# Weight loads in written order through the attention, 4,864-byte record rows, and output scatters that no longer wait for each other

## The chip, the cores and the metric

The kernel runs on one core of one Trainium2 chip. The metric is the device time of one execution in microseconds (us). Engines are named as in the profile: PE is TensorE, PEld its weight loads, DVE VectorE, ACT ScalarE, POOL GpSimd, SP SyncE, which only issues transfers here. "L157" is line 157 of the kernel before.

## The reference

Two stages. The first is attention over 8 batches, 12 heads, 448 positions and 64 dimensions with RMS-normalised q and k. The second is a mixture of 8 experts over the 3,584 token rows of 768 values that the attention gives: each row passes a dense two-layer network and one expert, chosen by its largest logit and scaled by that expert's softmax weight.

```python
q_n, k_n = rmsnorm(q, g_q), rmsnorm(k, g_k)
attn = softmax(q_n @ k_n.T / 8)            # per batch and head
x = (attn @ v) as rows (batch, position) of 768
y = relu(x @ w1_dense) @ w2_dense
e = argmax(x @ w_gate);  p = softmax(x @ w_gate)[e]
y += p * (relu(x @ w1[e]) @ w2[e])
```

## The kernel before

**Attention (to about 348 us).** The work is cut into 48 pieces t, each of two heads of one batch, six to a batch; two pieces make a group g of four heads. `load(g)` fetches q and k of a group (448 KB each, issued by SP, L137) and v (issued by POOL, with a cast to bf16, L141) into three buffers each. `squares(t)` multiplies x by itself on POOL (L157), and DVE sums the squares (L158). ACT makes the scale r of the group, `normalise(t)` applies it on DVE (L173), and `transposes(t)` turns q and k with PE (L182). `scores(t, j)` makes four blocks of scores with PE (L198), and ACT exponentiates each (L200): four such activations are one piece. `attend` multiplies by v (L211), and DVE divides into the row tile `xa` (L217). `values(g)` copies v into its own tile on DVE (L148).

One loop over t mixes these: scores of t+1, transposes of t+2, squares of t+4, normalise of t+3, load of group t/2+3 at each even t. Between them it works off, a few matmuls at a time, the dense network of the batch before (`dense1`, L265, `dense2`, L276). At the end of a batch `route(b)` makes the logits and writes the batch's rows to a table "records" in DRAM (L255, L256); `dense2` writes the dense result of each row beside them (L285).

The expert weights are 16 loads (`wjobs[3:]`, L321), two per expert, issued by POOL with a cast from float32 to bf16 (768 KB each after it). The loop names them at t = 3, 5, 8, 10, 13 and so on to 40:

```python
while nw < len(wjobs) and (nw - 2) * 5 <= t * 2:
    nc.gpsimd.dma_start(*wjobs[nw])
    nw += 1
```

The order on the engines is made by a scheduler ahead of time: only PE keeps the written order (`tc.manual_schedule(engines={PE})`). On the other engines, SP's and POOL's transfers among them, the scheduler puts forward what it holds to be ready; each engine then works through its list in that order, and an instruction that waits holds up all behind it.

**Dispatch (348 to 373 us).** DVE works out the slot of each token: 35 tiles of 128 slots, each tile of one expert.

**Experts (from 373 us).** For tile t, `gather(t)` fetches its 128 rows from the records (POOL, indirect, L441) into `xg`, which has five buffers. PE transposes them (L452), multiplies by the first weights (L461), transposes again (L471) and multiplies by the second (L479). DVE adds the dense result of the same record into `ys` (L485), and POOL scatters the 128 rows to the output (indirect, L487). Gather t+5 needs the buffer that the addition of tile t frees. The scatters all write one DRAM tensor at rows that are known only at run time, so the tracking of dependencies makes each wait until the one before has landed.

A row of the records is 385 float32 words (768 bf16 values and one word with the gate) and 768 words of the dense result: 1,153 words, 4,612 bytes.

Of the kernel before, what the change touches and what calls it, by code (L numbers as in the profile page):

```python
# [8 lines left out]
F32 = mybir.dt.float32  # L9
BF16 = mybir.dt.bfloat16  # L10
# [7 lines left out]
def kernel(  # L18
# [14 lines left out]
    nc = tc.nc  # L33
    P = 128
    B, H, S, D = q.shape
    N = B * S
    Dm = H * D
# [3 lines left out]
    SC = S // JJ  # L41
# [23 lines left out]

    EB = E * KD * F
    NTL = N // P + E - 1
    RW = Dm + 2
    NC4 = 4 * B
    tri = const.tile([P, P], BF16)  # L70
    ones = const.tile([P, P], BF16)
# [30 lines left out]
        nc.vector.tensor_copy(tok[:, b, :, 2], colp)  # L102
    nc.vector.memset(tok[:D, :, 3, :], 0.0)

    RC = RW // 2 + Dm
    rec = nc.dram_tensor("records", (N, RC), F32).ap()
    oh = const.tile([P, B, 4, E], BF16)
    wgb = const.tile([P, KD, E], BF16)
# [13 lines left out]
    with tc.tile_pool(name="a_ld", bufs=3) as ld, \  # L122
         tc.tile_pool(name="a_sb", bufs=2) as sb, \
         tc.tile_pool(name="a_sc", bufs=2, space=bass.MemoryType.PSUM) as scp, \
         tc.tile_pool(name="a_wk", bufs=4, space=bass.MemoryType.PSUM) as wkp:
        xin, ssqs, rs, xn, qkT, exs, vas, xnats, xTs, hTs, vrs = [{} for _ in range(11)]

        def load(g):
# [73 lines left out]
        def attend(t, hh):  # L202

            b, pr = divmod(t, NPR)
            if pr == 0 and hh == 0:
                xnats[b] = sb.tile([P, 4, RW], BF16, tag="xa", name="xa")
                xTs[b] = sb.tile([P, NPR, S], BF16, tag="xT", name="xT")
            av = wkp.tile([P, 4, De], F32, tag="wk", name="av")
            for mi in range(4):
                for j in range(JJ):  # L210
                    nc.tensor.matmul(av[:, mi], exs[t][:, j, hh, QC[mi]:QC[mi] + P],  # L211
                                     vas[t // GP][:, 2 * (t % GP) + hh, j, :De],
                                     start=(j == 0), stop=(j == JJ - 1))
            inv = sb.tile([P, 4, 1], F32, tag="inv")
            nc.vector.reciprocal(inv, av[:, :, D:])
            h = 2 * pr + hh
            nc.vector.tensor_mul(xnats[b][:, :, h * D:(h + 1) * D], av[:, :, :D],  # L217
                                 inv.to_broadcast([P, 4, D]))
# [11 lines left out]
        def route(b):  # L230

            lp = wkp.tile([P, 4, E], F32, tag="wk", name="tr")
            for mi in range(4):
                for kk in range(KD):
                    nc.tensor.matmul(lp[:, mi], xTs[b][:, kk, QC[mi]:QC[mi] + P], wgb[:, kk, :],
                                     start=(kk == 0), stop=(kk == KD - 1))
            mx = sb.tile([P, 4, 1], F32, tag="mx")
            nc.vector.tensor_reduce(mx, lp, AX.X, ALU.max)
            cent = sb.tile([P, 4, E], F32, tag="cent")
            nc.vector.tensor_sub(cent, lp, mx.to_broadcast([P, 4, E]))  # L240
            eg = sb.tile([P, 4, E], F32, tag="eg")
            nc.scalar.activation(eg, cent, AF.Exp)

            hot = sb.tile([P, 4, E], F32, tag="hot")
            nc.vector.scalar_tensor_tensor(hot, in0=cent, scalar=0.0,
                                           in1=prio.unsqueeze(1).to_broadcast([P, 4, E]),
                                           op0=ALU.is_equal, op1=ALU.mult)
            m2 = sb.tile([P, 4, 1], F32, tag="m2")
            nc.vector.tensor_reduce(m2, hot, AX.X, ALU.max)
            nc.vector.tensor_tensor(oh[:, b], hot, m2.to_broadcast([P, 4, E]), ALU.is_equal)  # L250
            sm = sb.tile([P, 4, 1], F32, tag="sm")
            nc.vector.tensor_reduce(sm, eg, AX.X, ALU.add)
            nc.vector.reciprocal(xnats[b][:, :, Dm:].bitcast(F32), sm)
            dst = rec[b * S:b * S + 3 * P, :RW // 2].rearrange("(m p) w -> p m w", p=P)
            nc.sync.dma_start(dst, xnats[b][:, :3].bitcast(F32))  # L255
            nc.sync.dma_start(rec[b * S + 3 * P:(b + 1) * S, :RW // 2], xnats[b][D:, 3].bitcast(F32))  # L256


        def dense1(b, ff, part, n=3):
# [10 lines left out]
        def dense2(b, j, dd, part, n=2):  # L270
            if part == 0:
                if dd == 0:
                    ffs[1] = sb.tile([SC, 2, Dm // 2], F32, tag="ys", name="ys")
                ffs[0] = wkp.tile([SC, Dm // 2], F32, tag="wk", name="ff")
            for ff in range(part * FT // n, (part + 1) * FT // n):
                nc.tensor.matmul(ffs[0], hTs[b][:, ff, j * SC:(j + 1) * SC],  # L276
                                 wd2[:, ff, dd * Dm // 2:(dd + 1) * Dm // 2],
                                 start=(ff == 0), stop=(ff == FT - 1))
            if part == n - 1:
                if dd == 0:  # L280
                    nc.scalar.copy(ffs[1][:, dd], ffs[0])
                else:
                    nc.vector.tensor_copy(ffs[1][:, dd], ffs[0])
                    r0 = b * S + j * SC
                    nc.sync.dma_start(rec[r0:r0 + SC, RW // 2:],  # L285
                                      ffs[1].rearrange("p a d -> p (a d)"))

        ffs = [None, None]
# [8 lines left out]
                for f, *args in PIECES[n * len(PIECES) // NSL:(n + 1) * len(PIECES) // NSL]:  # L297
                    f(b - 1, *args)

        with tc.manual_schedule(engines={mybir.EngineType.PE}):  # L300
            for g in range(3):
                load(g)
            for job in wjobs[:3]:
                nc.gpsimd.dma_start(*job)
            for t in range(2 * GP):
                squares(t)
            values(0)
            for t in range(3):
                normalise(t)
            for t in range(2):  # L310
                transposes(t, "q")
                transposes(t, "k")
            for j in range(JJ):
                scores(0, j)
            nw = 3
            for t in range(NT + NPR):
                if t < NT:
                    if t % GP == 0:
                        load(t // GP + 3)
# [3 lines that stand above are left out]
                for i in range(4):  # L323
                    if t + 1 < NT:
                        scores(t + 1, i)
                    if i % 2 == 0:
                        if t + 2 < NT:
                            transposes(t + 2, "qk"[i // 2])
                        if i == 2 and 0 < t <= NT:
                            xtrans(t - 1)  # L330
                    elif t < NT:
                        attend(t, i // 2)
                    dense(t, i)
                    if i < 2:
                        if t + 2 * GP < NT:
                            squares(t + 2 * GP, "qk"[i])
                    elif t + 3 < NT:
                        normalise(t + 3, "qk"[i - 2])
                    if i == 3 and t % GP == GP - 1 and t + 1 < NT:
                        values((t + 1) // GP)  # L340

    with tc.tile_pool(name="m_sb", bufs=5) as sb, \
# [94 lines left out]
        xgs = {}  # L437
# [8 lines left out]
        xTs, hes, heTs = {}, {}, {}  # L446

        def xtrans(t):
            xb = xgs[t][:, :Dm // 2].bitcast(BF16)
            xp = ps1.tile([P, KD, P], BF16, tag="tr")  # L450
            for kk in range(KD):
                nc.tensor.transpose(xp[:, kk], xb[:, kk * P:(kk + 1) * P], ident)  # L452
            xTs[t] = sb.tile([P, KD, P], BF16, tag="xT", name="xT")
            nc.vector.tensor_copy(xTs[t], xp)  # L454

        def gemm1(t):
            gate = xgs[t][:, Dm // 2:RW // 2]
            eregs[t] = nc.tensor.value_load(tei[:, t:t + 1], min_val=0, max_val=E - 1)
            he = ps2.tile([P, F], F32, tag="he")
            for kk in range(KD):  # L460
                nc.tensor.matmul(he, xTs[t][:, kk],  # L461
                                 we[:, bass.ds(eregs[t], 1), 0, kk * F:(kk + 1) * F]
                                 .rearrange("p o f -> p (o f)"),
                                 start=(kk == 0), stop=(kk == KD - 1))
            hes[t] = sb.tile([P, F], BF16, tag="hs", name="hs")
            nc.scalar.activation(hes[t], he, AF.Relu, scale=gate)  # L466
# [8 lines left out]
        def gemm2(t):  # L475
            yp = psy.tile([P, 2, 512], F32, tag="y")
            for ff in range(FT):
                for dd in range(2):
# [4 lines left out]
                                     start=(ff == 0), stop=(ff == FT - 1))  # L483
            ys = sb.tile([P, 2, HD], F32, tag="ys")
            nc.vector.tensor_add(ys, yp[:, :, :HD],  # L485
                                 xgs[t][:, RW // 2:].rearrange("p (a d) -> p a d", a=2))
            nc.gpsimd.indirect_dma_start(  # L487
                out=out, out_offset=bass.IndirectOffsetOnAxis(ap=dest[:, t:t + 1], axis=0),
                in_=ys.rearrange("p a d -> p (a d)"), in_offset=None,
                bounds_check=N - 1, oob_is_err=False)  # L490

        eregs = {}
        for t in range(4):
            gather(t)
        with tc.manual_schedule(engines={mybir.EngineType.PE}):
# [44 lines left out]
```

## Time and profile before

| | us |
|---|---|
| median of 3 runs (lowest, highest) | 540.01 (537.35, 541.17) |
| the profiled execution | 539.3 |
| its span in the profile | 537.3 |

The span is the time from the first to the last instruction of the profiled execution; 2.0 us lie around it. All stretches below are in us from the start of the span. Mean granted clock of TensorE over it: 0.903 of 2.4 GHz.

### The profile page before, as it was taken

To read this page: it belongs to the slowest core of one execution; us is meant where nothing else is said; L and a number is where in the kernel's file an instruction comes from. 1 tells how busy PE (TensorE), PEld (TensorE's weight loads), DVE (VectorE), ACT (ScalarE), POOL (GpSimd) and SP (SyncE) were. 2 spreads that over 40 slices of the span, in tenths; PEclk is the share of its full clock that TensorE was granted. 3 is DMA by queue.
4 is the path that set the end of the run, shared out by engine and by line. 5 is a ranking of instruction groups with operands and counts; after the bars stand their busy time and mean duration, and the time that the engine had idled before them with its cause. 6 is when DMAs were issued, how large, how long until landed. Compare 5 with 4: busy or idle time off the path is not lost. (4 is left out here: it accounts for less than half of the span.)

```text
span 537.3 us, 10725 instructions
## 1 busy us (share of the span) xinstructions
PE 401.6 (75%) x3995; PEld 232.5 (43%) x4010; DVE 319.0 (59%) x759; ACT 273.8 (51%) x431; POOL 207.1 (39%) x223
## 2 busy tenths in 40 slices
PE   0198891769889898888898999802597877878882
PEld 0155550445454454554554656502254444445441
DVE  3899780968977786786887854275143433334331
ACT  0088582557677777776778888300132333223320
POOL 6785542625433444343333000001244544444432
PEclk9998586788898999898899999956699999899997
DMA  8999999999576465555563312410556766677650
GB/s 149 236 243 233 235 241 238 217 266 234 118 169 149 111 165 139 135 142 138 138 154 107 93 63 73 144 43 8 213 177 201 234 228 196 207 239 230 232 180 26
DMA packets 62176, 90.58 MB, mean 169 GB/s; under 512 B 4909, under 2 KB 52269, under 8 KB 62128
## 3 DMA queue, kind: packets, MB, share of 16 engines
q0 software_dynamic: 31568, 51.36, 41.2%
q1 hardware_dynamic: 30560, 38.56, 25.0%
q8 instruction: 33, 0.54, 0.4%
q14 instruction: 15, 0.12, 0.1%
HBM read 82.03 MB, written 30.29 MB: 209 GB/s over the span
## 5 line engine op out<-in xcount | busy, mean ns | idle before, releaser
L200 ACT ACTIVATE ex<-ps 112x896 bf16<-112x896 f32 x192 | 174.0, 921 | 60.0 <-PE ps L198 59.1
L198 PE MATMUL ps<-y 64*112 64x448 bf16 x384 | 84.4, 437 | 3.8 <-ACT ex L200 2.1
L158 DVE TENSOR_REDUCE ssq<-sq 112x8 f32<-112x512 f32 x96 | 64.3, 673 | 34.3 <-POOL sq L157 34.2
L157 POOL TENSOR_TENSOR sq<-xq 112x512 f32<-112x512 f32 x48 | 50.8, 1058 | 84.0 <-DMA xq<-in_q_dram 51.9
L211 PE MATMUL av<-va,ex 112*128 112x65 bf16 x1536 | 71.2, 202 | 11.5 <-DVE xa L217 8.7
L276 PE MATMUL ff<-wd,hT 128*112 128x384 bf16 x256 | 62.4, 356 | 15.8 <-DVE xa L217 15.6
L211 PEld LDWEIGHTS <-ex 112*128 112x128 bf16 x1536 | 59.1, 103 | 34.0 <-issue 20.7
L441 POOL DMA_INDIRECT xg<-records,row x35 | 33.9, 968 | 91.7 <-DVE dest L434 81.3
L487 POOL DMA_INDIRECT out_dram<-ys,dest x35 | 35.7, 1019 | 79.4 <-DVE ys L485 28.5
L157 POOL TENSOR_TENSOR sq<-xk 112x512 f32<-112x512 f32 x48 | 54.0, 1125 | 30.1 <-DMA xk<-in_k_dram 15.4
L454 DVE COPY xT<-xp 128x768 bf16<-128x768 bf16 x35 | 19.5, 558 | 73.8 <-PE xp L452 69.8
L182 PE MATMUL tr<-ident,y 112*128 112x112 bf16 x384 | 39.7, 233 | 27.1 <-DVE y L173 24.5
L473 ACT COPY heT<-hp 128x512 bf16<-128x512 bf16 x35 | 20.5, 585 | 69.3 <-PE hp L471 69.3
L466 ACT ACTIVATE hs<-he,xg 128x512 bf16<-128x512 f32 x35 | 24.1, 687 | 62.3 <-DMA xg<-records,row 35.5
L198 PEld LDWEIGHTS <-y 64*112 64x112 bf16 x384 | 26.5, 132 | 63.1 <-issue 51.2
L479 PE MATMUL yp<-we,heT 128*128 x280 | 52.3, 331 | 0.8 <-DVE ys L485 0.8
L461 PE MATMUL he<-we,xT 128*128 x195 | 50.5, 384 | 2.8 <-DVE xT L454 0.8
L265 PE MATMUL ff<-xT,wd 128*128 128x448 bf16 x192 | 50.6, 367 | 2.6 <-DVE xa L217 2.6
L485 DVE TENSOR_TENSOR ys<-yp,xg 128x768 f32<-128x768 f32 x35 | 33.5, 958 | 28.9 <-PE yp L479 28.9
L182 PEld LDWEIGHTS <-y 112*128 112x128 bf16 x384 | 22.8, 105 | 49.8 <-DVE y L173 27.3
L173 DVE TENSOR_TENSOR y<-xq,r 112x512 bf16<-112x512 f32 x48 | 42.5, 886 | 0.8 <-ACT r L164 0.7
L452 PE MATMUL xp<-ident,xg 128*128 128x128 bf16 x210 | 18.6, 228 | 31.5 <-DMA xg<-records,row 23.4
(97 smaller groups left out, 490.1 us busy)
## 6 DMA issues: line engine op xcount, KB each, us to landing
we<-in_moe_w_dram POOLq DMA_DIRECT2D x16, 768.0 KB, 33.5
records<-ys SPq DMA_DIRECT2D x32, 336.0 KB, 3.6
xq<-in_q_dram SPq DMA_DIRECT2D x23, 448.0 KB, 6.1
xk<-in_k_dram SPq DMA_DIRECT2D x23, 448.0 KB, 5.7
vr<-in_v_dram POOLq DMA_DIRECT2D x24, 224.0 KB, 4.9
records<-xa SPq DMA_DIRECT2D x8, 577.5 KB, 4.1
wd<-in_moe_w_dense_dram POOLq DMA_DIRECT2D x2, 768.0 KB
records<-xa SPq DMA_DIRECT2D x8, 96.2 KB, 4.4
```

The source lines that it names most:

```text
L157: nc.gpsimd.tensor_mul(sq, x, x)
L158: nc.vector.tensor_reduce(ssqs[g][:, n, 2 * i * JJ:(2 * i + 2) * JJ], sq.rearrange("p h (j d) -> p (h j) d", d=D), AX.X, ALU.add)
L173: nc.vector.tensor_mul(y.rearrange("p j h d -> p h j d"), x.rearrange("p h (j d) -> p h j d", d=D), rs[g][:, n, 2 * i * JJ:(2 * i + 2) * J ...
L182: nc.tensor.transpose(ps[:, j * SC:(j + 1) * SC], xn[name, t][:, j].rearrange("p h d -> p (h d)"), ident[:SC, :SC])
L198: nc.tensor.matmul(ps[:, hh, :S], qkT["k", t][d0:d0 + D, j * SC:(j + 1) * SC], qkT["q", t][d0:d0 + D, :], start=True, stop=True)
L200: nc.scalar.activation(exs[t][:, j], ps[:, :, :S], AF.Exp, scale=scale)
L211: nc.tensor.matmul(av[:, mi], exs[t][:, j, hh, QC[mi]:QC[mi] + P], vas[t // GP][:, 2 * (t % GP) + hh, j, :De], start=(j == 0), stop=(j == ...
L265: nc.tensor.matmul(ffs[0], wd1[:, kk, ff * P:(ff + 1) * P], xTs[b][:, kk], start=(kk == 0), stop=(kk == KD - 1))
L276: nc.tensor.matmul(ffs[0], hTs[b][:, ff, j * SC:(j + 1) * SC], wd2[:, ff, dd * Dm // 2:(dd + 1) * Dm // 2], start=(ff == 0), stop=(ff == F ...
L461: nc.tensor.matmul(he, xTs[t][:, kk], we[:, bass.ds(eregs[t], 1), 0, kk * F:(kk + 1) * F] .rearrange("p o f -> p (o f)"), start=(kk == 0), ...
L479: nc.tensor.matmul(yp[:, dd, :HD], heTs[t][:, ff], we[:, bass.ds(eregs[t], 1), 1, ff * Dm + dd * HD:ff * Dm + (dd + 1) * HD] .rearrange("p ...
L487: nc.gpsimd.indirect_dma_start(out=out, out_offset=bass.IndirectOffsetOnAxis(ap=dest[:, t:t + 1], axis=0), in_=ys.rearrange("p a d -> p (a ...
```

## The change

- SP and POOL join PE in the manual schedule of the attention: their instructions, transfers too, are issued as the loop writes them. The weight loads so go out at t = 3, 5, 8, ..., 40.
- A record row becomes 384 words of x, 768 words of the dense result, and 64 words whose first is the gate: 1,216 words, 4,864 bytes. x, the dense result and the tail begin at bytes 0, 1,536 and 4,608 of the row.
- The gate is no longer part of the `xa` tile. It goes into one of two small tiles `gt`, and `route` writes their 256-byte rows with two transfers more per batch (16 in all).
- Each output scatter is declared free of the earlier ones.

```diff
-    RW = Dm + 2
+    XH = Dm // 2
+    GO = XH + Dm
...
-    RC = RW // 2 + Dm
+    RC = Dm // 2 + Dm + 64
...
+        gts = [sb.tile([P, 4, RC - GO], F32, name=f'gt{i}', tag=f'gt{i}', bufs=1) for i in range(2)]
+        for gt in gts:
+            nc.vector.memset(gt, 0.0)
...
-                xnats[b] = sb.tile([P, 4, RW], BF16, tag="xa", name="xa")
+                xnats[b] = sb.tile([P, 4, Dm], BF16, tag="xa", name="xa")
...
-            nc.vector.reciprocal(xnats[b][:, :, Dm:].bitcast(F32), sm)
-            dst = rec[b * S:b * S + 3 * P, :RW // 2].rearrange("(m p) w -> p m w", p=P)
-            nc.sync.dma_start(dst, xnats[b][:, :3].bitcast(F32))
-            nc.sync.dma_start(rec[b * S + 3 * P:(b + 1) * S, :RW // 2], xnats[b][D:, 3].bitcast(F32))
+            gt = gts[b % 2]
+            nc.vector.reciprocal(gt[:, :, :1], sm)
+            r3 = b * S + 3 * P
+            nc.sync.dma_start(rec[b * S:r3, :XH].rearrange("(m p) w -> p m w", p=P),
+                              xnats[b][:, :3].bitcast(F32))
+            nc.sync.dma_start(rec[r3:r3 + D, :XH], xnats[b][D:, 3].bitcast(F32))
+            nc.sync.dma_start(rec[b * S:r3, GO:].rearrange("(m p) w -> p m w", p=P), gt[:, :3])
+            nc.sync.dma_start(rec[r3:r3 + D, GO:], gt[D:, 3])
...
-                    nc.sync.dma_start(rec[r0:r0 + SC, RW // 2:],
+                    nc.sync.dma_start(rec[r0:r0 + SC, XH:GO],
...
-        with tc.manual_schedule(engines={mybir.EngineType.PE}):
+        with tc.manual_schedule(engines={mybir.EngineType.PE, mybir.EngineType.Pool, mybir.EngineType.SP}):
...
-            nc.gpsimd.indirect_dma_start(
+            i = nc.gpsimd.indirect_dma_start(
                 out=out, out_offset=bass.IndirectOffsetOnAxis(ap=dest[:, t:t + 1], axis=0),
...
+            for j in stores:
+                tc.declare_no_dep(i.ins, j.ins, reason="each token has one slot")
+            stores.append(i)
```

The expert stage reads the parts of a record at their new places; its schedule is as before (PE alone in written order).

## Rows read from the trace of the kernel before

**Rows 1.** Busy time by stretch: engines' busy us (instructions), granted clock, DMA share, GB/s.

```profile
20.00:95.00 75.00, 54.12 (x564) 31.80 (x564) 54.11 (x121) 45.16 (x68) 39.28 (x43) 0.80 1.18 237
130.00:260.00 130.00, 113.27 (x1309) 64.17 (x1308) 102.24 (x262) 96.11 (x155) 53.96 (x53) 0.93 0.59 141
399.00:520.00 121.00, 96.78 (x671) 54.43 (x681) 43.40 (x57) 36.21 (x57) 56.73 (x57) 0.99 0.66 220
```

**Rows 2.** The activations of L200 by stretch: ACT busy (count), clock, DMA share, GB/s.

```profile
55.00:126.00 71.00, 29.44 (x33) 0.72 1.18 240
126.00:268.00 142.00, 79.95 (x89) 0.93 0.61 146
```

**Rows 3.** PE in order of time, 81.8 to 96 us: start, length, line, [idle before].

```profile
82.13 0.68 PE L211 MATMUL av<-va,ex 112*128 112x65 bf16 x16
95.28 0.89 PE L276 MATMUL ff<-wd,hT 128*112 128x384 bf16 x2 [12.47 <-DVE xa L217]
```

**Rows 4.** DVE in order of time, 85 to 95 us.

```profile
94.47 0.43 DVE L148 COPY va<-vr 112x1024 bf16<-112x1024 bf16 x1 [9.12 <-DMA vr<-in_v_dram]
```

**Rows 5.** Transfers issued in 20 to 95 us: count, KB each, median us to landing.

```profile
we<-in_moe_w_dram POOLq DMA_DIRECT2D x16, 768.0 KB, 33.5
xq<-in_q_dram SPq DMA_DIRECT2D x6, 448.0 KB, 8.8
xk<-in_k_dram SPq DMA_DIRECT2D x6, 448.0 KB, 12.2
```

**Rows 6.** Transfers issued in 130 to 260 us.

```profile
xq<-in_q_dram SPq DMA_DIRECT2D x10, 448.0 KB, 4.4
xk<-in_k_dram SPq DMA_DIRECT2D x10, 448.0 KB, 5.2
```

**Rows 7.** Waits of DVE, 20 to 130 us: us in total, times, longest.

```profile
DVE ssq L158 <- POOL sq L157: 4.8, 2, 4.2
```

**Rows 8.** Waits of DVE and of PE, 130 to 260 us.

```profile
DVE ssq L158 <- POOL sq L157: 22.2, 19, 3.3
...
PE av L211 <- DVE xa L217: 7.6, 6, 2.1
```

**Rows 9.** POOL in order of time, 373 to 537 us: first scatter, a scatter and gather in the middle, last.

```profile
391.05 1.04 POOL L487 DMA_INDIRECT out_dram<-ys,dest  x1 [11.50 <-DVE ys L485]
...
424.81 1.02 POOL L487 DMA_INDIRECT out_dram<-ys,dest  x1 [1.59 <-DMA out_dram<-ys,dest]
426.13 0.97 POOL L441 DMA_INDIRECT xg<-records,row  x1 [0.30 <-issue]
...
531.81 0.98 POOL L487 DMA_INDIRECT out_dram<-ys,dest  x1 [1.88 <-DMA out_dram<-ys,dest]
```

**Rows 10.** The output tensor: scatters from issue to landing, least, median, most.

```profile
DMA to landing us min/median/max: 3.1/4.4/4.7
```

**Rows 11.** PE in order of time, 386 to 432 us.

```profile
386.68 1.46 PE L461 MATMUL he<-we,xT 128*128 x6 [0.41 <-PE hp L471]
...
399.29 1.46 PE L461 MATMUL he<-we,xT 128*128 x5
401.76 0.51 PE L452 MATMUL xp<-ident,xg 128*128 128x128 bf16 x6 [1.02 <-DMA xg<-records,row]
...
430.63 0.51 PE L452 MATMUL xp<-ident,xg 128*128 128x128 bf16 x6 [0.27 <-issue]
430.98 1.46 PE L479 MATMUL yp<-we,heT 128*128 x8
```

**Rows 12.** DVE in order of time, 420 to 432 us.

```profile
424.65 0.96 DVE L485 TENSOR_TENSOR ys<-yp,xg 128x768 f32<-128x768 f32 x1 [0.74 <-PE yp L479]
```

**Rows 13.** Waits of all engines, 399 to 520 us.

```profile
PEld L452 <- DMA xg<-records,row: 35.7, 26, 3.5
```

**Rows 14.** SP's queue in order of time, 120 to 170 us.

```profile
165.88 0.39 SPq L255 DMA_DIRECT2D records<-xa  x1
166.32 0.49 SPq L256 DMA_DIRECT2D records<-xa  x1
```

More of the change, by code (lines that the diff above doesn't have):

```diff
@@ L448, in xtrans @@
         def xtrans(t):
-            xb = xgs[t][:, :Dm // 2].bitcast(BF16)
+            xb = xgs[t][:, :XH].bitcast(BF16)
             xp = ps1.tile([P, KD, P], BF16, tag="tr")
@@ L456, in gemm1 @@
         def gemm1(t):
-            gate = xgs[t][:, Dm // 2:RW // 2]
+            gate = xgs[t][:, GO:GO + 1]
             eregs[t] = nc.tensor.value_load(tei[:, t:t + 1], min_val=0, max_val=E - 1)
@@ L485, in gemm2 @@
             nc.vector.tensor_add(ys, yp[:, :, :HD],
-                                 xgs[t][:, RW // 2:].rearrange("p (a d) -> p a d", a=2))
-            nc.gpsimd.indirect_dma_start(
+                                 xgs[t][:, XH:GO].rearrange("p (a d) -> p a d", a=2))
+            i = nc.gpsimd.indirect_dma_start(
                 out=out, out_offset=bass.IndirectOffsetOnAxis(ap=dest[:, t:t + 1], axis=0),
@@ L490, in gemm2 @@
                 bounds_check=N - 1, oob_is_err=False)
-        eregs = {}
+            for j in stores:
+                tc.declare_no_dep(i.ins, j.ins, reason="each token has one slot")
+            stores.append(i)
+        eregs, stores = {}, []
         for t in range(4):
```

## The prediction

> **What bounds the kernel now.** I read the busy time by stretch first, since the mean over the span hides three stages. In 399 to 520 us, the experts, no engine is full: PE 96.78 of 121 us, POOL 56.73, DMA share 0.66 [rows 1]. The waits of this stretch say why PE stands still: its transposes wait for gathers, 35.7 us in 26 times on the load side [rows 13]. POOL in order of time says why the gathers are late. From the first scatter at 391.05 to the last at 531.81 lie 34 intervals [rows 9], so 140.76 / 34 = 4.14 us each. A scatter lands 4.4 us (median) after its issue [rows 10], and the next one waits for that; the gather of five tiles on stands behind it in POOL's list. The wait before the scatter at 424.81 is put down to the scatter before [rows 9]. What PE could do is seen while it lived on the five gathers made ahead: from 386.68 to 399.29 it did four tiles [rows 11], 3.15 us each. So the expert stage is bounded by the scatters' chain, with PE 1 us per tile behind it.
>
> The attention is read by its activations, four to a piece. 89 of them in 126 to 268 us are 22.25 pieces, 6.38 us each; 33 in 55 to 126 us are 8.25 pieces, 8.6 us each [rows 2]. In the second stretch the DMA share is 1.18 against 0.61. All 16 weight loads are issued between 20 and 95 us and take 33.5 us to land; q and k land after 8.8 and 12.2 us there, against 4.4 and 5.2 us in 130 to 260 us [rows 5, 6]. The worst of it is one hole: PE stops from 82.8 to 95.28 us, 12.47 us [rows 3], because DVE stood 9.12 us in front of the copy of v, whose transfer POOL had issued behind weight loads [rows 4]. The granted clock averages 0.72 over the stretch and 0.93 later [rows 2]. Even the later stretch is not bound by one full engine: DVE waits 22.2 us in 19 times for squares, and PE 7.6 us for what DVE then delivers late [rows 8].
>
> **The change, part by part.** *Scatters unchained.* What is late next is a ring over three tiles: addition of tile t, scatter, gather of t+5, its transposes, the second product three tiles on, its addition. From the rows: 0.30 us to issue, 1.32 from scatter to gather (424.81 to 426.13) [rows 9], L from gather to transposes, 4.50 here (426.13 to 430.63) [rows 9, 11], 0.35 to the second product, 1.46 for it [rows 11], 0.96 for the addition [rows 12]: 4.39 + L = 8.89 us, or 2.96 per tile. PE's 3.15 is then the bound, by only 0.19 us. POOL's own need is about two issues of 1 us and two gaps of 0.3, 2.6 us, which fits. But L was read at a DMA share of 0.66 [rows 1]; at 3.3 us per tile the share is 0.66 x 4.14 / 3.3 = 0.83, and more with the wider rows, against the 1.18 at which it is full. I take L = 5.5, one us more, so (4.39 + 5.5) / 3 = 3.30 us. Ends: 3.15 (PE) and L = 7.0, 3.80. Gain: 140.76 - 34 x 3.30 = 28.6 us, ends 33.7 and 11.6.
>
> *Wider, aligned rows.* The gather moves 4,864 for 4,612 bytes, 5.5% more. Of the 2.7 us of share per tile (0.66 x 4.14) the gather is more than half; 5.5% of at most 2.7 us is under 0.15 us in L, 0.05 us per tile, within the choice above. The Trainium skill, DMA: Bandwidth & Descriptors, section "How a descriptor splits into AXI transactions", says that a row that does not begin on a 256-byte boundary fetches the bytes before it too. By that rule, 4,864 aligned bytes take 19 transactions and the old rows 19 or 20, so the widening costs nothing and L would not grow; no row of this trace separates the two, and the sum would move by under 2 us.
>
> *The tail transfers.* 16 more issues on SP. The two records issues of L255 and L256 take 0.38 and 0.49 us of the queue [rows 14]; as much again for each batch delays a load behind them by about 0.9 us, eight times. Nobody waits for a record before the first gather. I count nothing; without that cover, 7 us. Clearing `gt` and the shorter `xa` are under 1 us of DVE at the start, while it waits for the first loads.
>
> *Weights in written order, what is removed.* No transfer of v stands behind a row of weight loads any more, and q and k have the DMA to themselves until t = 3. The stretch 55 to 126 us at the later pace takes 8.25 x 6.38 = 52.6 us for 71: gain 18.4 us. The hole with its low clock is most of that.
>
> *What it adds.* 14 of the 16 loads (t of 8 and more) now run beside q and k in a stretch that had none. Bounds per load: nothing, since in the crowded 20 to 130 us DVE waited for squares only 4.8 us in all [rows 7], though q and k landed 4.4 and 7.0 us later there than in the open stretch [rows 5, 6]; and 7.0 us, if the full lateness of k reaches DVE, as DVE's list is in order and the transposed tiles, divisions and copies PE waits for are queued behind the waiting sum of squares. I take 0.5 us, near the lower end, because the row of the crowded stretch is the nearest: half of the loads meet a group's transfers, and a meeting costs one wait of the usual size, 22.2 / 19 = 1.2 us [rows 8]. 14 x 0.5 = 7 us lost, ends 0 and 98.
>
> *Written order on SP and POOL itself.* A load of q and k is now issued behind the records writes that stand before it, so as much as one piece, 6.4 us, later than its buffer allows; it is written six pieces before the piece it feeds, and what must follow (landing 5 us, four squares of 1 us, sums, scale, normalise) needs about 15 of some 25 us. On POOL the squares stand behind the weight loads' issues, under 1 us each. I count nothing for either; if that cover is gone, each us of lateness falls on DVE as above.
>
> The Trainium skill, same page, section "Queues, rings and completion order", says that each DMA engine takes packets from the queues in turn. By that rule SP's loads would share the engines with a weight load however it is placed, and the weights' cost would only be moved into the open stretch: attention gain 0. The landing times fit the sharing [rows 5, 6], but the hole came from waiting within POOL's own queue [rows 4], which the spreading removes.
>
> **Sum.** 537.3 us of span and 2.0 around it, 539.3, less 28.6, less 18.4, plus 7: 499.3. The median of the runs, 540.0, is 0.7 above the profiled execution: 500 us.
>
> **The rivals.**
> - *PE binds the experts and the attention gains more.* L stays at 4.5, and the new lists put the sums of squares later, so that PE's waits of 7.6 us and part of the clock come back. 540 - 33.7 - 18.4 - 7.6 = 480; down to 476. For it: PE's unbroken run at 3.15 us. Against: DMA share 0.83 and more.
> - *The gather ring binds.* Scatters and gathers in flight together bring L to 7: gain 11.6 for 28.6, 517.
> - *The weights' cost is only moved.* Loads late by sharing eat what the hole gives back, 18.4: 540 - 28.6 = 511; by 1.3 us per load. For it: those 22.2 us of waits show how little reserve the open stretch has. Against: [rows 7].
> - *The scatters still wait*, for a semaphore or a buffer: 540 - 18.4 + 7 = 529. `ys` has five buffers, so I see no reason.
> - *Slower: DVE stalls behind late loads.* Place: the sum of squares (L158) of each group that meets a weight load. Price: 7.0 us, what k landed later beside weights [rows 5, 6], for 16 loads, 112 us: 540 - 47 + 112 = 605. It decides from 47 / 16 = 2.9 us per load on; the usual wait of 1.2 us [rows 8] speaks against.
>
> **How the numbers follow.** Forecast (490 to 509) 0.44; the first rival 0.22; the ring 0.12; cost only moved 0.10; scatters still wait 0.05; slower 0.07. The range 477 to 520 holds the forecast and three rivals, 0.85 with some of the first rival's low end outside. Runs of this kernel spread by 0.7%, so 1% is about what a measurement can tell from no change. Faster by over 1%: 0.90. Within 1%: 0.04. Slower: 0.06.
>
> **What would show it.** Scatters 3.2 to 3.4 us apart, none waiting for a scatter, and PE's transposes hardly waiting. The DMA share spread evenly, near 0.8 to 0.9 up to some 290 us; no wait of DVE for v; no hole at 83 us; about 6.4 us a piece from 55 us to the end of the weights. Wrong would be: DVE's waits for squares grown past 50 us, or scatters over 3.8 us apart.

## The result, and the profile after

| | before | after |
|---|---|---|
| median, us (4 runs each) | 540.29 | 519.23 |
| lowest, highest | 537.35, 541.17 | 518.21, 521.35 |
| profiled execution, its span | 539.3, 537.3 | 519.15, 517.3 |

The ratio after to before is 0.962 (95% interval 0.958 to 0.967): 20 us faster. Some executions of a kernel come out one to three per cent longer than its others: the ratios leave them out, the medians do not, and three traces that caught such a one (the order alone, the loads written earlier, the last kernel) are not read. 500 was forecast, with a range from 477 to 520. The forecast gave the expert stage 28.6 us and the attention 11.4 net. Busy time by stretch (as in rows 1) and POOL in order of time show what came of the first.

```profile
399.00:500.00 101.00, 93.03 (x687) 55.07 (x686) 43.24 (x58) 36.46 (x58) 56.71 (x57) 1.00 0.82 274
```

```profile
393.26 1.04 POOL L495 DMA_INDIRECT out_dram<-ys,dest  x1 [13.26 <-DVE ys L493]
...
396.42 1.01 POOL L495 DMA_INDIRECT out_dram<-ys,dest  x1 [0.84 <-DVE ys L493]
397.73 0.96 POOL L449 DMA_INDIRECT xg<-records,row  x1 [0.30 <-ACT hs L474]
...
511.74 0.98 POOL L495 DMA_INDIRECT out_dram<-ys,dest  x1 [1.53 <-DVE ys L493]
```

The first and the last scatter are 118.48 us apart, for 140.76 before [rows 9]: 3.485 us per tile in place of 4.14. No scatter waits for a scatter any more; each waits for its own addition. The DMA share rose from 0.66 [rows 1] to 0.82. PE is busy 92% of the stretch but not all of it, as it still meets late gathers. PE in order of time, and the waits in 400 to 500 us:

```profile
404.57 0.51 PE L460 MATMUL xp<-ident,xg 128*128 128x128 bf16 x6 [1.60 <-DMA xg<-records,row]
```

```profile
PEld L460 <- DMA xg<-records,row: 11.1, 10, 2.1
```

These transposes belong to the gather issued at 397.73: 6.84 us from issue to use, where the row before had 4.50 [rows 9, 11]. The gathers of the whole stage land after 6.0 us (median, transfers by issue):

```profile
xg<-records,row POOLq DMA_INDIRECT x35, 6.0
```

The attention shows a gain and its loss. The activations of the scores by stretch (ACT busy, count, clock, DMA share, GB/s), their first and last start (the kernel before, then the changed one), and PE's longest wait between 80 and 97 us:

```profile
55.00:126.00 71.00, 40.53 (x46) 0.95 0.84 172
126.00:268.00 142.00, 74.69 (x83) 0.90 0.87 183
```

```profile
L200 ACT ACTIVATE ex<-ps x192: 896/917/995, 27.2 to 332.0; 112x896 bf16<-112x896 f32 x192
```

```profile
L204 ACT ACTIVATE ex<-ps x192: 896/917/1007, 28.1 to 332.0; 112x896 bf16<-112x896 f32 x192
```

```profile
96.15 0.68 PE L215 MATMUL av<-va,ex 112*128 112x65 bf16 x16 [1.56 <-DVE xa L221]
```

In 55 to 126 us there are 46 activations for 33 before [rows 2]: the hole of 12.47 us at 83 us is gone, and the granted clock is 0.95 for 0.72. At the later pace before of 1.6 us each, 13 more are worth 21 us. In 126 to 268 us there are 83 for 89, and the others are lost before 55 and behind 268 us. The last one starts at 332.0, as it did in the kernel before, so by the end of the attention all of it has been given back. That the two agree so closely is chance.

POOL's waits in 20 to 330 us show where; the first line is of the kernel before, the second of the changed one:

```profile
POOL sq L157 <- DMA xq<-in_q_dram: 50.6, 11, 7.6
```

```profile
POOL sq L161 <- DMA xq<-in_q_dram: 117.4, 12, 12.1
```

SP's queue in order of time:

```profile
126.48 0.60 SPq L141 DMA_DIRECT2D xq<-in_q_dram  x1
...
129.37 14.39 SPq L293 DMA_DIRECT2D records<-ys  x3
144.28 0.33 SPq L141 DMA_DIRECT2D xq<-in_q_dram  x1
...
145.66 1.25 SPq L260 DMA_DIRECT2D records<-xa  x1
...
148.20 0.39 SPq L263 DMA_DIRECT2D records<-gt  x1
148.64 0.79 SPq L264 DMA_DIRECT2D records<-gt  x1
149.53 1.42 SPq L141 DMA_DIRECT2D xq<-in_q_dram  x1
```

The load at 144.28 goes out right after the third of three records writes, which SP issued over 14.39 us; the next follows after 5.25 us, behind the writes of `route`. The pattern repeats in each batch: gaps of about 18, 16 and 5 us.

One load shows the whole way from SP to PE. DVE, SP, POOL and PE in order of time, then a stretch by engine with the granted clock behind the busy times:

```profile
84.92 0.68 DVE L177 TENSOR_TENSOR y<-xq,r 112x512 bf16<-112x512 f32 x1
...
109.41 0.69 DVE L162 TENSOR_REDUCE ssq<-sq 112x8 f32<-112x512 f32 x1 [4.22 <-POOL sq L161]
```

```profile
88.75 12.15 SPq L293 DMA_DIRECT2D records<-ys  x3
100.99 0.98 SPq L141 DMA_DIRECT2D xq<-in_q_dram  x1
```

```profile
108.35 1.03 POOL L161 TENSOR_TENSOR sq<-xq 112x512 f32<-112x512 f32 x1 [9.75 <-DMA xq<-in_q_dram]
```

```profile
112.61 1.06 PE L215 MATMUL av<-va,ex 112*128 112x65 bf16 x16 [4.40 <-DVE xa L221]
```

```profile
110.40:117.20 6.80, 4.59 (x38) 2.37 (x39) 6.25 (x13) 1.53 (x3) 5.77 (x7) 0.50 1.14 228
```

The normalise at 84.92 is the last reader of the buffer that the load of 100.99 fills, so the buffer is free at 85.60; the load goes out 15.4 us later, right after three records writes. POOL stands 9.75 us for it, DVE 4.22 us for POOL's square, and PE 4.40 us for a division that stands behind the sum of that square on DVE's list. While PE stands, from 108.21 to 112.61, the granted clock falls to 0.50, the 1.2 GHz level, and stays there until 117.20.

### The profile page after: what moved, and what is told of

It reads as the page before. It is cut to its first block, busy times and chain, and to the rows that moved or that the text cites. A ratio compares the mean times of both kernels' runs of the same rounds, so it can differ in the third digit from the quotient of the medians.

```text
span 517.3 us, 10774 instructions
## 1 busy us (share of the span) xinstructions
PE 399.3 (77%) x4010; PEld 232.7 (45%) x4010; DVE 326.6 (63%) x761; ACT 274.8 (53%) x431; POOL 205.3 (40%) x223
## 4 chain that ended last, share of the span: by engine, by line
PE 30%; DMA 27%; DVE 20%; ACT 7%; issue 6%; POOL 6%; SPq 2%; POOLq 0%; DVEq 0%; ACTq 0%
DMA xq<-in_q_dram 9%; DMA xg<-records,row 9%; DMA xk<-in_k_dram 8%; DVE y L177 7%; PE he L469 5%; PE av L215 5%; DVE ssq L162 5%; PE ps L202 5%; PE yp L487 4%; ACT ex L204 4%; POOL sq L161 4%; PE ff L273 4%; PE ff L284 2%; DVE xa L221 2%; PE tr L186 2%
## 5 line engine op out<-in xcount | busy, mean ns | idle before, releaser
L161 POOL TENSOR_TENSOR sq<-xq 112x512 f32<-112x512 f32 x48 | 52.1, 1085 | 141.8 <-DMA xq<-in_q_dram 118.8
L284 PE MATMUL ff<-wd,hT 128*112 128x384 bf16 x256 | 60.4, 347 | 10.8 <-DVE xa L221 10.8
L161 POOL TENSOR_TENSOR sq<-xk 112x512 f32<-112x512 f32 x48 | 51.3, 1070 | 19.1 <-DVE ssq L162 9.8
L469 PE MATMUL he<-we,xT 128*128 x210 | 53.5, 393 | 3.0 <-issue 1.5
L273 PE MATMUL ff<-xT,wd 128*128 128x448 bf16 x192 | 52.1, 373 | 2.1 <-DVE xa L221 2.1
L487 PE MATMUL yp<-we,heT 128*128 x280 | 51.2, 326 | 0.8 <-DVE ys L493 0.8
L177 DVE TENSOR_TENSOR y<-xq,r 112x512 bf16<-112x512 f32 x48 | 45.0, 937 | 0.9 <-ACT r L168 0.9
L221 DVE TENSOR_TENSOR xa<-av,inv 128x256 bf16<-128x256 f32 x96 | 40.1, 418 | 1.4
```

Source lines behind the costliest of these rows:

```text
L161: nc.gpsimd.tensor_mul(sq, x, x)
L177: nc.vector.tensor_mul(y.rearrange("p j h d -> p h j d"), x.rearrange("p h (j d) -> p h j d", d=D), rs[g][:, n, 2 * i * JJ:(2 * i + 2) * J ...
L273: nc.tensor.matmul(ffs[0], wd1[:, kk, ff * P:(ff + 1) * P], xTs[b][:, kk], start=(kk == 0), stop=(kk == KD - 1))
L469: nc.tensor.matmul(he, xTs[t][:, kk], we[:, bass.ds(eregs[t], 1), 0, kk * F:(kk + 1) * F] .rearrange("p o f -> p (o f)"), start=(kk == 0), ...
L487: nc.tensor.matmul(yp[:, dd, :HD], heTs[t][:, ff], we[:, bass.ds(eregs[t], 1), 1, ff * Dm + dd * HD:ff * Dm + (dd + 1) * HD] .rearrange("p ...
```

## The experiments

Ratios are to the kernel before, run beside each on the same chip; a difference of 0.01 in the ratio is 5.4 us. The theory at the start: the scatters give all of the gain, and the written order gives back in the attention what the removed hole brought. The rivals: the aligned rows carry a part, or the weight loads beside q and k give it back, whatever SP does.

**Unchained scatters alone**, on the kernel before.

```diff
-            nc.gpsimd.indirect_dma_start(
+            i = nc.gpsimd.indirect_dma_start(
...
+            for j in stores:
+                tc.declare_no_dep(i.ins, j.ins, reason="each token has one slot")
+            stores.append(i)
...
-        eregs = {}
+        eregs, stores = {}, []
```

> The kernel before with the scatters declared free of each other, nothing else. Theory (all of the gain comes from the scatters): first to last scatter shrinks from 140.8 us to about the 118.5 us of the changed kernel, so 540 - 22 = 518 us. Rival (the aligned rows carry part of it): over 522 us, scatters 3.6 us apart or more.

Measured: 522.34 us, ratio 0.963 (0.955 to 0.971). First and last scatter:

```profile
395.16 1.04 POOL L487 DMA_INDIRECT out_dram<-ys,dest  x1 [13.76 <-DVE ys L485]
...
512.53 0.98 POOL L487 DMA_INDIRECT out_dram<-ys,dest  x1 [1.53 <-DVE ys L485]
```

117.37 us, 3.45 per tile. The declaration alone is worth as much as the whole change. The aligned rows do not bring the scatters closer: with them the interval is 3.485 us.

**The order alone**, on the kernel before.

```diff
-        with tc.manual_schedule(engines={mybir.EngineType.PE}):
+        with tc.manual_schedule(engines={mybir.EngineType.PE, mybir.EngineType.Pool, mybir.EngineType.SP}):
```

> The kernel before with POOL and SP in written order in the attention, nothing else. Theory (the order removes the hole at 83 us and gives as much back later): 540 us within 1%, the last activation of the scores near 328 us. The prediction's own figure for the order, 18.4 gained and 7 lost: 529 us.

Measured: 539.4 us, ratio 0.994 (0.990 to 0.998): within 1%, as the theory has it, and not the 529 of the prediction's terms.

**No order**: the changed kernel with PE alone in written order.

```diff
-        with tc.manual_schedule(engines={mybir.EngineType.PE, mybir.EngineType.Pool, mybir.EngineType.SP}):
+        with tc.manual_schedule(engines={mybir.EngineType.PE}):
```

> The changed kernel with PE alone in written order: aligned rows and free scatters remain. Theory: like the unchained kernel alone, 518 us, with the hole at 83 us back. Rival (aligned rows shorten the gathers): 3 us or more below the unchained kernel alone, from the expert stage.

Measured: 530.58 us, ratio 0.973 (0.966 to 0.979): a miss for both. By the ratios it is 5 us slower than the unchained kernel alone, with intervals that overlap.

**POOL in order, SP free.**

```diff
-        with tc.manual_schedule(engines={mybir.EngineType.PE, mybir.EngineType.Pool, mybir.EngineType.SP}):
+        with tc.manual_schedule(engines={mybir.EngineType.PE, mybir.EngineType.Pool}):
```

> The changed kernel with PE and POOL in written order, SP left to the scheduler: the weight loads are spread, but the loads of q and k need not stand behind the records writes. Theory (SP's order gives the gain back): 503 to 510 us, pieces of 6.4 us while weights load. Rival (weight loads beside q and k give it back, whatever SP's order): 519 us within 1%, pieces of 7.1 us.

Measured: 502.86 us, ratio 0.927 (0.920 to 0.933), which is 500.7 us beside 540.3. So SP's order costs (0.962 - 0.927) x 540 = 19 us. Its activations, first and last, and POOL's and DVE's waits from the 14th to the 40th piece (103 to 273 us; the changed kernel's lie in 104 to 289 us and stand below these; those of the kernel before lie in 125 to 291 us):

```profile
L204 ACT ACTIVATE ex<-ps x192: 897/917/1051, 27.8 to 313.6; 112x896 bf16<-112x896 f32 x192
```

```profile
POOL vr L145 <- DVE va L152: 41.0, 10, 5.7
POOL sq L161 <- DMA xq<-in_q_dram: 16.8, 7, 7.8
...
DVE ssq L162 <- POOL sq L161: 23.3, 18, 4.9
```

```profile
POOL sq L161 <- DMA xq<-in_q_dram: 99.1, 10, 12.1
...
DVE ssq L162 <- POOL sq L161: 34.6, 12, 6.3
```

The attention ends 18.4 us sooner (313.6 for 332.0), with the weight loads spread as in the changed kernel. POOL's waits for q fall from 99.1 to 16.8 us; in their place it stands 41.0 us for buffers of v that DVE's copy has yet to free, which did not keep the attention from ending sooner. The rival that blamed the weight loads falls.

The same 26 pieces, PE first: the changed kernel, this run, the kernel before.

```profile
104.00:289.00 185.00, 153.11 (x1700) 85.71 (x1699) 139.25 (x339) 124.93 (x198) 76.81 (x80) 0.89 0.88 185
```

```profile
103.00:273.00 170.00, 142.23 (x1684) 80.47 (x1681) 139.39 (x343) 122.52 (x198) 79.69 (x81) 0.95 0.89 195
```

```profile
125.00:291.00 166.00, 145.76 (x1694) 82.50 (x1692) 130.44 (x336) 123.69 (x198) 68.82 (x69) 0.94 0.61 147
```

A piece takes 7.1 us in the changed kernel, 6.5 with SP free, 6.4 before. Of the 15 us between the first two, PE's idle time is 4 (31.9 for 27.8); 11 are longer busy time for the same matmuls, at a mean granted clock of 0.89 for 0.95.

**SP in order, POOL free**: the fourth corner.

```diff
-        with tc.manual_schedule(engines={mybir.EngineType.PE, mybir.EngineType.Pool, mybir.EngineType.SP}):
+        with tc.manual_schedule(engines={mybir.EngineType.PE, mybir.EngineType.SP}):
```

> The changed kernel with PE and SP in written order, POOL left to the scheduler, so that the weight loads go out early again: the fourth corner beside none (0.97 of the kernel before), POOL alone (0.93) and both (0.96). If SP's order costs the same whatever the weights do, 18 us: 545 us, the hole at 83 us back. If it costs only beside spread weight loads: 527 us within 5.

Measured: 539.62 us, ratio 0.996 (0.993 to 1.000). The wait of DVE for v is back (60 to 130 us):

```profile
DVE va L152 <- DMA vr<-in_v_dram: 7.1, 1, 7.1
```

| the new rows and free scatters, and in written order: | ratio |
|---|---|
| PE | 0.973 |
| PE and POOL | 0.927 |
| PE and SP | 0.996 |
| PE, POOL and SP (the change) | 0.962 |

POOL's order gains 0.034 with SP in order and 0.046 with it free, 18 to 25 us. SP's order loses 0.024 with POOL free, 0.036 with POOL in order, 13 to 19 us. So it costs with early weight loads too; whether it costs less there is within the noise of four ratios, and the first row of the table is the one that came out slower than the unchained kernel alone (0.963).

**Loads one piece earlier**, POOL and SP in order.

```diff
-                    if t % GP == 0:
-                        load(t // GP + 3)
+                    if t % GP == 1 or t == 0:
+                        load((t + 1) // GP + 3)
```

> The changed kernel, SP and POOL still in written order, with each load of a group written one piece earlier, ahead of the records writes of that piece. Theory (the loads of q and k come late because they stand behind records writes on SP): POOL's 99 us of waits for q shrink to under 40, and the time falls to that of the kernel with SP left free, 503 us within 5. Rival (it is the fixed order of SP as such, or the weight loads): 515 us or more.

Measured: 537.72 us, ratio 0.987 (0.983 to 0.991): 13 us slower than the change, where the theory had 16 us faster. In the written order, moving the loads ahead of one set of records writes puts them behind another (a load of t = 6k + 1 stands right behind the writes of `route`), so this edit does not take the writes out of their way. That writing a load earlier cures it is refuted. The edit also moves the load of v, which POOL issues, ahead of the copy (`values`, written at the end of that piece) that frees its buffer, with squares standing behind it on POOL's list; that this is why it is slower still is not shown.

**Records writes on ACT**, so that SP's list holds loads alone, still in written order (five issues changed as this one).

```diff
-                    nc.sync.dma_start(rec[r0:r0 + SC, XH:GO],
+                    nc.scalar.dma_start(rec[r0:r0 + SC, XH:GO],
```

> The changed kernel, SP and POOL in written order, with the records writes issued by ACT, so that SP's list holds loads alone. Theory (on SP the loads stand behind records writes, come in pairs with gaps of 18 us between, and meet a list of DVE that expects them sooner): loads about 12 us apart, 503 us within 6. Rival (SP's order without the writes costs as much): 515 us or more.

Measured: 505.86 us, ratio 0.931 (0.923 to 0.940). POOL's and DVE's waits, 103 to 273 us:

```profile
POOL sq L161 <- DMA xq<-in_q_dram: 8.7, 3, 4.1
...
DVE ssq L162 <- POOL sq L161: 3.7, 4, 1.8
```

Taking the writes out of SP's list gives 17 of the 19 us back, with SP still in written order. The waits for q and for squares are gone, too. The loads are not 12 us apart, though; their gaps are still uneven (SP's queue, then a line of DVE before the third of these loads):

```profile
120.18 0.31 SPq L141 DMA_DIRECT2D xq<-in_q_dram  x1
...
132.83 0.31 SPq L141 DMA_DIRECT2D xq<-in_q_dram  x1
...
151.72 0.31 SPq L141 DMA_DIRECT2D xq<-in_q_dram  x1
...
156.79 0.31 SPq L141 DMA_DIRECT2D xq<-in_q_dram  x1
```

```profile
150.98 0.67 DVE L177 TENSOR_TENSOR y<-xq,r 112x512 bf16<-112x512 f32 x1
```

So uneven gaps do not explain the loss. What differs is the time from the free buffer to the load: the normalise at 150.98 ends at 151.65, and the load goes out at 151.72. For the loads of groups 7 to 20 this time is 13.5 us on average in the changed kernel (3.6 to 20.8), and 0.1 us in this one, with SP free, and in the kernel before.

**DVE in written order too.**

```diff
-        with tc.manual_schedule(engines={mybir.EngineType.PE, mybir.EngineType.Pool, mybir.EngineType.SP}):
+        with tc.manual_schedule(engines={mybir.EngineType.PE, mybir.EngineType.Pool, mybir.EngineType.SP,
+                                        mybir.EngineType.DVE}):
```

> The changed kernel with DVE in written order too, beside PE, POOL and SP. Theory (DVE's list, made by the scheduler for loads that land sooner than they do, puts the sums of squares too far ahead, and DVE stands in front of them): the 34.6 us of waits for squares between the 14th and the 40th piece fall under 10, and the time to 505 us or less. Rival (DVE's order is not the matter, or its written order stalls elsewhere): 515 us or more, with other waits in the place of these.

Measured: 552.44 us, ratio 1.015 (1.011 to 1.020). The waits for squares remain, and POOL now stands for the copy of v (103 to 300 us):

```profile
DVE ssq L162 <- POOL sq L161: 29.6, 14, 2.6
...
POOL vr L145 <- DVE va L152: 113.7, 13, 10.3
```

The rival holds: with DVE in written order the waits are elsewhere, so whether the place of the sums in DVE's list carries SP's loss is not settled by it.

**Weight loads doubled**, on POOL in order and SP free.

```diff
                         nc.gpsimd.dma_start(*wjobs[nw])
+                        if nw + 2 < len(wjobs):
+                            nc.gpsimd.dma_start(wjobs[nw + 2][0], wjobs[nw][1])
```

> The changed kernel with SP left free, and 14 of the 16 weight loads issued a second time, to a place that a later load overwrites: twice the weight traffic beside q and k. The prediction's 0.5 us per load: 7 us more, 510 us. The upper bound of 7.0 us per load: 600 us. Nothing per load: 503 us.

Measured: 523.89 us, ratio 0.968 (0.963 to 0.973): 22 us more than without the second 14, 1.6 us each. The transfers issued in 130 to 260 us, with the doubled loads, then with the single ones:

```profile
xq<-in_q_dram SPq DMA_DIRECT2D x9, 448.0 KB, 9.8
xk<-in_k_dram SPq DMA_DIRECT2D x8, 448.0 KB, 10.3
```

```profile
xk<-in_k_dram SPq DMA_DIRECT2D x10, 448.0 KB, 5.4
xq<-in_q_dram SPq DMA_DIRECT2D x9, 448.0 KB, 4.6
```

The second set doubles the landing time of q and k. In this stretch the first set hardly moved it: 4.4 and 5.2 us without weight loads [rows 6]. It is not always so: issued in 60 to 130 us of the kernel with single loads they take 7.6 and 7.3 us, and in 130 to 260 us of the changed kernel 6.3 and 7.0.

**Old rows**: the kernel before with free scatters, as in the first run, and POOL in order.

```diff
-        with tc.manual_schedule(engines={mybir.EngineType.PE}):
+        with tc.manual_schedule(engines={mybir.EngineType.PE, mybir.EngineType.Pool}):
```

> The kernel before with free scatters and POOL in written order: 4,612-byte rows, the gate in the row tile, no tail transfers, SP free. If the new rows cost nothing and gain nothing: 503 us within 1%, as the same with the new rows. If the tail transfers on SP cost what the kernel with new rows and no order lost against the unchained one, 8 us: 495. If the aligned rows gain in the expert stage: 506 or more.

Measured: 501.54 us, ratio 0.926 (0.920 to 0.933), the same as with the new rows (0.927), within about 4 us to each side. Any cost of the wider rows and the tail transfers is below that. The traces hint at a small one: the scatters are 3.42 us apart here and 3.45 in the first run, both with old rows, and 3.485 to 3.56 in the traces with new rows and five buffers (1 to 5 us over the stage); each kernel has one trace, so this is not shown. The 5 us by which the new rows were slower with no order at all stay open: both lists of SP and POOL are the scheduler's there and come out differently.

**Seven buffers for gathered rows**, on POOL in order and SP free; gathers go six tiles ahead.

```diff
-        xg = sb.tile([P, RC], F32, tag="xg", name="xg")
+        xg = sb.tile([P, RC], F32, tag="xg", name="xg", bufs=7)
...
-        for t in range(4):
+        for t in range(6):
...
-                if t + 4 < NTL:
-                    gather(t + 4)
+                if t + 6 < NTL:
+                    gather(t + 6)
```

> The changed kernel with SP left free, and seven buffers for gathered rows in place of five, with gathers six tiles ahead. Theory (a ring over three tiles, 4.39 us and a landing time of 6.1, sets 3.5 us per tile): the ring then runs over five tiles, PE is the bound at 3.15 to 3.2, scatters 3.2 us apart, 34 x 0.3 = 10 us less: 493 us. Rival (the transfers themselves are the bound): scatters stay 3.45 or more apart, 501 us or more.

Measured: 490.58 us, ratio 0.905 (0.899 to 0.910), the fastest kernel here. First and last scatter with five buffers (POOL in order, SP free), then with seven, and 385 to 475 us by engine with seven:

```profile
374.65 1.04 POOL L495 DMA_INDIRECT out_dram<-ys,dest  x1 [13.47 <-DVE ys L493]
...
495.67 0.98 POOL L495 DMA_INDIRECT out_dram<-ys,dest  x1 [1.53 <-DVE ys L493]
```

```profile
375.23 1.04 POOL L495 DMA_INDIRECT out_dram<-ys,dest  x1 [10.74 <-DVE ys L493]
...
481.53 0.98 POOL L495 DMA_INDIRECT out_dram<-ys,dest  x1 [1.52 <-DVE ys L493]
```

```profile
385.00:475.00 90.00, 89.37 (x678) 55.19 (x688) 43.01 (x58) 36.37 (x57) 53.47 (x54) 1.00 0.87 290
```

106.3 us for 121.0, 3.13 per tile for 3.56, and PE is busy 89.37 of 90 us: PE is the bound, and the DMA carries 290 GB/s without being one. The ring theory holds, the transfer theory falls.

**All three together**: POOL in order with SP free, records writes on ACT, seven buffers. Edits as above.

> Three findings together: POOL in written order with SP free, records writes issued by ACT, seven buffers of gathered rows. If the writes on ACT add to a free SP list: under 488 us. If SP's free list already has what they give: 490 us, as without them.

Measured: 498.61 us, ratio 0.916 (0.909 to 0.923). Slower than without the writes on ACT (0.905) by the median, though the intervals touch, and under 488 us is refuted. With SP free the writes on ACT give nothing; whether they cost something stays open.

## Why the prediction was right or wrong

**Scatters: right mechanism, L too small.** The chain went, and the ring of three tiles took its place, as forecast. The term that was mis-sized is L: taken as 5.5 us, it is 3 x 3.485 - 4.39 = 6.1, and the gathers landed after 6.0 us. So the gain was 22.3 us for 28.6. The stage also began 2.2 us later by its first scatter. The ring itself was shown by seven buffers, which bring 3.13 us; 3.15 had been read off PE. With the attention's 11.4 us net, of which nothing was left, the 6.3 and the 2.2 make up the 20 us that the forecast was too low.

**Hole: right.** Forecast 18.4 us for 55 to 126 us; the 13 more activations are worth 21. In the corners POOL's order gives 18 to 25 us.

**Weights beside q and k: not the place of the loss.** With SP free, the attention ended 18.4 us sooner than before, more than the 18.4 - 7 = 11.4 forecast. The same 26 pieces took 170 us for 166 before, so the 14 loads cost some 4 us by these traces, where 7 had been taken; in the kernel with seven buffers, whose attention is the same, it was 173, so 0.5 us each is not refuted. A second set costs 1.6 each, at a DMA share of 1.06 for 0.91. The Trainium skill's rule of turns among the queues (DMA: Bandwidth & Descriptors, "Queues, rings and completion order") had made a rival of the moved cost, 511 us. The attention did end with gain 0, but by SP's order and not by that sharing, as the kernel with SP free has the same loads.

**Written order on SP: the step that failed.** The prediction said "I count nothing for either", as a load had some 25 us and needed about 15. It measured 19 us. The prediction let a load go out one piece, 6.4 us, later than its buffer allows; it was 13.5 us on average. And it reckoned the reserve up to the scores, six pieces behind the load, while the squares of a load are written only two pieces behind it (`squares(t + 4)` in the loop), where POOL, in order, stands until the load has landed. With records writes ahead of the loads on SP's list, POOL stands 99.1 us for q in place of 16.8, and DVE 34.6 us for squares in place of 23.3, in longer waits. Moving the writes off the list gave 17 us back, which shows the cause. The way from there to PE, by DVE's list and the granted clock, is shown for one load (84.92 to 117.20 us); that all of the loss goes this way is argued from the waits and not shown, and DVE in written order failed to isolate it.

**Rows: right, as far as the runs can tell.** The prediction bounded the widening at 0.05 us per tile and counted nothing for it. The ratios of old and new rows, 0.926 and 0.927, show no cost within about 4 us to each side; the scatters' intervals, 3.42 and 3.45 us for 3.485 to 3.56, hint at 0.03 to 0.14 us per tile. The Trainium skill's rule on descriptors that begin off a 256-byte boundary (same page, "How a descriptor splits into AXI transactions") had the widening cost nothing; the ratios agree and the intervals do not bear it out. By that rule the old rows take 19 transactions at any of their starts, and not the prediction's 19 or 20. The tail transfers were counted as nothing, too; the first of the two records issues took 0.39 us in its row, not 0.38.

The forecast of 500 is what the kernel with SP free measures, 500.7. The range held the 519.2 by luck: its upper end was there for the ring at L = 7 (517) and the moved cost of the weights (511), and neither happened; SP's order had no rival of its own.

## What to carry to other kernels

A list that is worked off in order holds back what stands behind a waiting transfer: before it is put into written order, ask of each load which write of unfinished work stands ahead of it, and give loads and late writes lists of their own. When a chain is removed, write down the ring that is next with its latency as a variable: the latency grew here with the load that the freed stage itself makes (4.5 us at a DMA share of 0.66, 6.1 at 0.82), and two buffers more took it off the path. A change of several parts is to be taken apart even if it wins: here one declaration carried the whole gain, and two other parts, one of +18 to 25 us and one of -13 to 19, cancelled.

## What the runs showed of the hardware that was not expected

Weight traffic beside q and k cost little until it was doubled: with SP free, at a DMA share of 0.91 in 130 to 260 us, q and k land in 4.6 and 5.4 us, while with a second set of weight loads, at 1.06 in the same stretch, they take 9.8 and 10.3 and the kernel loses 22 us.

A loss on PE need not show as idle time: of the 15 us that 26 pieces take longer with SP in order, 4 are idle time of PE, and 11 are its matmuls at a mean granted clock of 0.89 for 0.95. In the place shown, the clock fell to the lower level while PE stood 4.40 us and stayed there for 4.6 us behind it.
